# Splitting two of eight gate experts into two float32r parts, with an accumulating DMA that joins two output sums

## The chip, the cores and the metric

The kernel runs on one core of one Trainium2 chip. The metric is the device time of one execution in microseconds (us). Three runs of the kernel before gave 724.45, 724.79 and 724.89 us; their median, 724.79 us, is the time before. A separate execution was taken by the hardware profiler and is the source of every duration below.

## The reference, cut to what matters

The first half is a short dynamic convolution (seven taps, eight heads), the second a gated feed-forward layer. All of it is float32.

```python
w = softmax(weight_gen)                       # (4, 4160, 8, 7), over the 7 taps
out = einsum('bshk,bskhg->bshg', w, x_unf)    # x_unf: x at the 7 positions up to s; (4, 4160, 192)
h = maximum(out @ w_in, 0)                    # (4, 4160, 1024)
conv_out = sum_k conv_w[k] * h[s + k - 1]     # three taps along s, per channel
gate = 1 / (1 + exp(-conv_out))
result = (h * gate) @ w_out                   # (4, 4160, 192)
```

## The kernel before, in words

The 4 x 4160 positions are cut into 128 segments of 130 positions, one per partition. A **block** is four positions of every segment, so 512 tokens; there are 33 blocks (`NB`), the first with two positions of output and the others with four. The 1024 inner channels are eight groups of 128; the code calls one `f`, and it is called an expert here as in the change's title.

Each block goes through four stages:

1. **Attention** (`head`). Seven products of `x` (kept in a ring in SBUF) with the softmax weights, each 128 x 768, called taps (line 292), most on POOL. In the first three blocks TensorE transposes and adds all seven. From the fourth block on they are first folded: an accumulating DMA adds three pieces onto three others (`fold1`, line 315), a second one adds two onto two (`fold2`, line 318), POOL adds the last two (`fold3`, line 322), and TensorE transposes one piece, in two parts (line 327). POOL executes in order and issues both DMAs, so `fold2` waits on POOL until `fold1` has landed.
2. **First product** (`mm1`, line 359). The transposed block is split in a high and a low float32r part (lines 338 and 343). For each expert five float32r multiplications with 512 moving columns make `z`: one **unit**, eight a block.
3. **Gate** (lines 365 to 392). ACT takes the ReLU, ACT and VectorE make the three-tap convolution, ACT the tanh, and VectorE writes the gated value `g` (`gmul`) into an SBUF buffer of all eight experts.
4. **Second product** (`mm2`, line 405). For each of the block's 128-token slices eight float32 multiplications, one per expert, `g` as the weights and 192 columns of `w_out` as the moving side: one **tile**. There are 2 + 32 x 4 = 130. ACT evacuates a tile (line 414), and SP stores a block (line 418). The trace shows a float32 multiplication as two rows, each with a weight load of its own: 130 x 8 x 2 = 2080 rows.

Before this the weights arrive in an eight-byte form and are decoded on ACT, VectorE and POOL, which takes the first stage of the program; POOL there waits for VectorE through small memsets (`tok`, lines 874 and 875).

The order of all instructions comes from a planner in the kernel: `task(engine, duration, dependencies)` collects the work, a list scheduler with priorities (`TO` for attention, `FO` for transposes, `WO_` for tiles, in blocks) and one pass from the end and one from the start order it, and each engine then executes its part in that fixed order. `PLAN` and `SMX` say which taps and softmax steps go to VectorE (V) or POOL (G), `CH` and `WOE` do so for the decoding, and `FORD` is the order of the experts in the first block.

Of the kernel before, what the change touches and what calls it, by code (L numbers as in the profile page):

```python
# [33 lines left out]
NY = 2  # L34
NZ = 5
# [3 lines left out]
CG = 2  # L39
CH = (  # L40
    ("f", 0, 256, 5.2, "VVS", "V"),
    ("m", 0, 256, 8.7, "VVS", "G"),
    ("f", 256, 512, 17.0, "GGP", "G"),
    ("m", 256, 512, 16.0, "VVS", "V"),
    ("m", 512, 1024, 18.0, "VVP", "V"),
)
# [19 lines left out]
def kernel(  # L66
# [49 lines left out]
    wo = const.tile([P, NF, D], F32, name="wo")  # L116
# [232 lines left out]
    def geom(j):  # L349
        no = R if j else R - 2  # L350
        return no, R + 1 - no
# [9 lines left out]
    def hrow(f, a, n):  # L361
        return h[:, f, a:a + n, :].rearrange("p s t -> p (s t)")
# [22 lines left out]
    def g_of(j, f):  # L385
        if j not in g_t:
            g_t[j] = g_p.tile([P, NF, W], F32, tag="g", name="g")
        return g_t[j][:, f, :geom(j)[0] * P]

    def gmul(j, f):  # L390
        no, cc = geom(j)
        nc.vector.scalar_tensor_tensor(  # L392
            out=g_of(j, f), in0=z_t[j, f][:, :no * P], scalar=1.0, in1=hrow(f, cc, no), op0=ALU.add, op1=ALU.mult
        )

    def carry(f0):
# [4 lines left out]
    def mm2(j, i, ps=None):  # L401
        if ps is None:
            ps = (ps_d if i % 2 else ps_o).tile([P, W], F32, tag="dps" if i % 2 else "ops", name="ops")
        for f in range(NF):
            nc.tensor.matmul(  # L405
                out=ps[:, 0:D], lhsT=g_of(j, f)[:, i * P:(i + 1) * P], rhs=wo[:, f, :],
                start=(f == 0), stop=(f == NF - 1),
            )
        return j, i, ps

    def evac(j, i, ps):
        if i == 0:
            o_t[j] = o_p.tile([P, R, D], F32, tag="o", name="o")
        nc.scalar.activation(out=o_t[j][:, i, :], in_=ps[:, 0:D], func=ACTF.Copy, scale=0.5)  # L414

    def store(j, a, b):
        c0 = R * j - 2 if j else 0
        nc.sync.dma_start(
            out=os_[:, (c0 + a) * D:(c0 + b) * D], in_=o_t[j][:, a:b].rearrange("p s d -> p (s d)")
        )  # L420

    V, G = nc.vector, nc.gpsimd

    with tc.manual_schedule():
        stage = g_p.tile([P, NF, W], I32, tag="g", name="stage").rearrange("p f w -> p (f w)")
        r_in = stage[:, 0:2 * FF].rearrange("p (c b) -> p c b", b=2)
        r_fold = stage[:, 2 * FF:3 * FF].rearrange("p (c b) -> p c b", b=2)
        r_cw = stage[0:3 * NF, 3 * FF:3 * FF + 2 * P].rearrange("p (c b) -> p c b", b=2)
        r_out = [o_p.tile([P, 2 * D, 2], I32, tag="o", name="r_out") for _ in range(4)]
        w_in_i = w_in.bitcast(I32).rearrange("k (f b) -> k f b", b=2)  # L430

        def load_in(eng, kind, a, b):
# [73 lines left out]
        def dma(occ, deps, fn):  # L506
            return task("none", 3.2, [task("H", occ, deps, fn)])
# [118 lines left out]
        wo_rdy = []  # L626
        for c in range(4):
            w = 2 * D
            iB, iC = ((1, 2), (4, 5))[c % 2]
            j_, _ = dec(  # L630
                wo[:, 2 * c:2 * c + 2].rearrange("p c d -> p (c d)").bitcast(I32), r_out[c],
                slots[iB][:, 0:w], slots[iC][:, 0:w], dma(1.6, spreads, lambda c=c: load_out(c)), used((iB, iC)), WOE[c],
            )
            last_use[iB] = last_use[iC] = [j_]
            wo_rdy.append(j_)


# [5 lines left out]
        def dadd(deps, occ, fn, e):  # L643
            return task("none", 3.2, [task("D", occ, [task("G", e, deps, fn)])])
# [9 lines left out]
        def head(q):  # L654
# [48 lines left out]
            if yend:  # L703
                yf_.append(task("none", 0.0, yend))

        zl, last_mm, mm_end = [], [None], {}

        def unit(j, f):
            n = j * NF + f
            so = 1 if j else 0  # L710
            now[0] = j + (FORD.index(f) if j == 0 else f) / NF
            mm[n] = task(
                "P", 1.135, spl_done[j] + w_rdy[f] + zl[-NZ:][:1] * (len(zl) >= NZ), lambda: mm1(j, f), after=[last_mm[0]])
            last_mm[0] = mm_end[j] = mm[n]
            m_ = geom(j)[0] * P
            r_ = task("A", act(W), [mm[n], ca.get(n - NF)] + ([] if j else [c2]), lambda: relu(j, f))
            y_ = task("A", act(m_, 1) + 0.04, [r_, c2], lambda: wmid(j, f))
            cv_ = task("V", vec(m_), [y_], lambda: conv_side(j, f, 2, 1))
# [3 lines left out]
            rd[n] = gm[n] = task("V", vec(m_, 0), [t_] + dep, lambda: gmul(j, f))  # L722
# [8 lines left out]
        zfree, last_evac, stored = [], [], []  # L731

        def out_tiles(j):
            d_ = 0.03 + NF * 0.326
            no = geom(j)[0]
            for i in range(no):
                now[0] = j + WO_ + i / R
                hold = {}
                z_ = j == NB - 1 and i % 2 == 0

                def fn(i=i, hold=hold, z_=z_):
                    hold[0] = mm2(j, i, ps_z.tile([P, W], F32, tag="z", name="z") if z_ else None)
                dep = [mm[NU - 1], (zl + zfree)[-NZ]] if z_ else bank[1 + i % 2]
                a_ = tiles[j, i] = task(
                    "P", d_, [rd[j * NF + f] for f in range(NF)] + wo_rdy + dep, fn,
                    after=[tiles.get((j, i - 1))])
                e_ = task("A", act(D) + 0.02, [a_] + (stored[-4:][:1] if i == 0 and len(stored) > 3 else []),
                          lambda hold=hold: evac(*hold[0]), begun=last_evac)
                last_evac[:] = [e_]
                if z_:  # L750
# [157 lines left out]
```

## Time and profile before

| | us |
|---|---|
| median of three runs | 724.79 |
| profiled execution, its own time | 722.55 |
| its span, first to last instruction | 720.8 |
| TensorE (PE) busy | 693.8 (96%) |
| VectorE (DVE) busy | 633.2 (88%) |
| ScalarE (ACT) busy | 546.9 (76%) |
| GpSimd (POOL) busy | 503.8 (70%) |

The span is 1.75 us shorter than that execution's own time, and that time is 2.24 us below the median. The granted TensorE clock was 0.998 of full speed over the span. A busy time is a union of recorded durations, which overlap from one instruction to the next, so the pace of an engine is better read from the distance between two starts.

### The profile page before, as it was taken

To read this page: it belongs to the slowest core of one execution; us is meant where nothing else is said; L and a number is where in the kernel's file an instruction comes from. 1 tells how busy PE (TensorE), PEld (TensorE's weight loads), DVE (VectorE), ACT (ScalarE), POOL (GpSimd) and SP (SyncE) were. 2 spreads that over 40 slices of the span, in tenths; PEclk is the share of its full clock that TensorE was granted. 3 is DMA by queue.
4 is the path that set the end of the run, shared out by engine and by line. 5 is a ranking of instruction groups with operands and counts; after the bars stand their busy time and mean duration, and the time that the engine had idled before them with its cause. 6 is when DMAs were issued, how large, how long until landed. Compare 5 with 4: busy or idle time off the path is not lost.

```text
span 720.8 us, 10895 instructions
## 1 busy us (share of the span) xinstructions
PE 693.8 (96%) x3809; PEld 630.0 (87%) x3809; DVE 633.2 (88%) x981; ACT 546.9 (76%) x1049; POOL 503.8 (70%) x390
## 2 busy tenths in 40 slices
PE   2799999899999999999999999999999999999998
PEld 1678898799999999999999999999999999999998
DVE  6999997899998989989898988999888888888882
ACT  3397887787878778878787787778777777787872
POOL 3588998969888789888777687887767767810000
PEclk9999999999999999999999999999999999999999
DMA  7635999997999888888898788878887886862111
GB/s 230 174 111 119 215 216 228 208 238 167 222 204 211 195 196 190 180 194 199 199 209 196 177 188 178 197 185 202 201 189 185 187 191 133 175 150 77 69 48 45
DMA packets 70787, 127.59 MB, mean 177 GB/s; under 512 B 5046, under 2 KB 42573, under 8 KB 70732
## 3 DMA queue, kind: packets, MB, share of 16 engines
q0 software_dynamic: 20160, 58.99, 47.0%
q1 hardware_dynamic: 50090, 67.51, 28.3%
q8 instruction: 30, 0.49, 0.3%
q10 hardware_dynamic: 482, 0.40, 0.2%
q14 instruction: 25, 0.20, 0.1%
HBM read 20.51 MB, written 12.78 MB: 46 GB/s over the span
## 4 chain that ended last, share of the span: by engine, by line
PE 82%; POOL 10%; DMA 4%; issue 2%; DVE 1%; ACT 1%; SPq 0%; POOLq 0%
PE ops L405 41%; PE z L359 36%; POOL py L292 4%; POOL px L292 4%; PE tp L327 3%; DMA px<-py 2%; DMA ring<-in_x_dram 1%; POOL px L318 1%; PE z L405 1%; DMA stage<-in_moe_w_in_dram 1%; POOL px L322 0%; POOL px L315 0%; DVE px L292 0%; POOL w L242 0%; SPq L437 0%
## 5 line engine op out<-in xcount | busy, mean ns | idle before, releaser
L376 DVE SCALAR_TENSOR_TENSOR z<-h,cw,z 128x512 f32<-128x512 f32 (+1 forms) x528 | 377.6, 741 | 14.7 <-ACT z L369 10.5
L405 PE MATMUL ops<-wo,g 128*128 128x192 f32 x2048 | 353.2, 326 | 0.0
L405 PEld LDWEIGHTS ops<-wo,g 128*128 128x128 f32 x2048 | 338.8, 190 | 10.2 <-DVE H L343 0.4
L359 PE MATMUL z<-H,wi 128*128 128x512 f32 x1056 | 304.3, 410 | 3.4 <-DVE g L392 3.4
L292 POOL TENSOR_TENSOR px<-ring,w 128x768 f32<-128x768 f32 (+2 forms) x141 | 229.6, 1774 | 66.8 <-PE tp L327 66.5
L359 PEld LDWEIGHTS z<-H,wi 128*128 128x128 f32 x1056 | 191.9, 189 | 35.6 <-DVE g L392 4.4
L392 DVE SCALAR_TENSOR_TENSOR g<-z,h 128x512 f32<-128x512 f32 (+1 forms) x264 | 179.5, 681 | 34.7 <-ACT z L383 32.0
L383 ACT ACTIVATE z<-z 128x512 f32<-128x512 f32 (+1 forms) x264 | 152.1, 577 | 61.7 <-DVE z L376 60.6
L369 ACT ACTIVATE z<-h,cw 128x512 f32<-128x512 f32 (+1 forms) x264 | 180.1, 683 | 5.4
L365 ACT ACTIVATE h<-z 128x512 f32<-128x512 f32 x264 | 156.0, 592 | 34.1 <-PE z L359 33.7
L292 POOL TENSOR_TENSOR py<-ring,w 128x768 f32<-128x768 f32 (+2 forms) x109 | 167.8, 1852 | 0.0
L359 PE MATMUL z<-L,wi 128*128 128x512 f32 x264 | 103.4, 392 | 0.0
L322 POOL TENSOR_TENSOR px<-px 128x768 f32<-128x768 f32 x30 | 68.2, 2275 | 8.5 <-DMA px<-px 8.5
L318 POOL DMA_DIRECT2D px<-px x30 | 38.3, 1275 | 31.5 <-DMA px<-py 31.2
L359 PEld LDWEIGHTS z<-L,wi 128*128 128x128 f32 x264 | 49.7, 188 | 11.4
L338 ACT ACTIVATE H<-tp 128x512 fp32r<-128x512 f32 (+1 forms) x63 | 37.2, 591 | 25.5 <-PE tp L327 25.3
L327 PE MATMUL tp<-ident,px 128*128 128x128 f32 (+1 forms) x288 | 45.5, 282 | 6.6 <-POOL px L292 3.5
L414 ACT ACTIVATE o<-ops 128x192 f32<-128x192 f32 x128 | 41.8, 326 | 10.6 <-PE ops L405 10.4
L327 PEld LDWEIGHTS tp<-ident,px 128*128 128x128 f32 (+1 forms) x288 | 34.4, 133 | 15.0 <-POOL px L292 5.5
L315 POOL DMA_DIRECT2D px<-py x30 | 42.7, 1424 | 6.4 <-POOL py L292 6.3
L343 DVE TENSOR_TENSOR L<-tp,H 128x512 fp32r<-128x512 f32 x33 | 22.7, 688 | 13.5 <-ACT H L338 13.4
L343 DVE TENSOR_TENSOR H<-tp,H 64x512 fp32r<-64x512 f32 x30 | 20.5, 683 | 2.2 <-ACT H L338 1.3
(81 smaller groups left out, 187.0 us busy)
## 6 DMA issues: line engine op xcount, KB each, us to landing
px<-py POOLq DMA_DIRECT2D x30, 1152.0 KB, 10.5
h<-h SPq DMA_DIRECT2D x128, 256.0 KB, 4.9
px<-px POOLq DMA_DIRECT2D x30, 768.0 KB, 6.8
ring<-in_x_dram SPq DMA_DIRECT2D x31, 384.0 KB, 7.9
out_dram<-o SPq DMA_DIRECT2D x31, 384.0 KB, 6.9
w<-in_weight_gen_dram SPq DMA_DIRECT2D x15, 224.0 KB, 7.2
r_out<-in_moe_w_out_dram SPq DMA_DIRECT2D x4, 384.0 KB, 5.3
wi<-scr SPq DMA_DIRECT2D x8, 128.0 KB, 5.8
```

Of the source, the lines that this page charges most:

```text
L292: eng.tensor_tensor(out=dst[:, a:b, :].rearrange("p s (h g) -> p s h g", g=GRP), in0=ring[:, p:p + n, :].rearrange("p s (h g) -> p s h g", ...
L318: nc.gpsimd.dma_start(out=fl4(px_t[q][:, 0:2]), in_=fl4(px_t[q][:, 2:4]), accum_op=ALU.add, max_dma_last_dim=3072)
L322: nc.gpsimd.tensor_tensor(out=a, in0=a, in1=b, op=ALU.add)
L327: nc.tensor.matmul(dst[0:D2 if part else P, c * P:(c + 1) * P], lhsT=src[:, c, part * P:part * D2 + P], rhs=ident, is_transpose=True, star ...
L343: nc.vector.tensor_tensor(out=H[D2:P, :] if part else h_t[q, "L1"], in0=tp[r, :], in1=H[r, :].bitcast(F32), op=ALU.subtract)
L359: nc.tensor.matmul(out=z, lhsT=w[:, fs], rhs=h_t[j, nm], start=(i == 0), stop=(i == len(terms) - 1))
L365: nc.scalar.activation(out=hrow(f, 2, R), in_=z_t[j, f], func=ACTF.Relu)
L369: nc.scalar.activation(out=z_t[j, f][:, :no * P], in_=hrow(f, cc, no), func=ACTF.Copy, scale=cw[:, NF + f:NF + f + 1])
L376: nc.vector.scalar_tensor_tensor(out=z, in0=hrow(f, cc + d, no), scalar=cw[:, k * NF + f:k * NF + f + 1], in1=z, op0=ALU.mult, op1=ALU.add,)
L383: nc.scalar.activation(out=z, in_=z, func=ACTF.Tanh, scale=0.5)
L392: nc.vector.scalar_tensor_tensor(out=g_of(j, f), in0=z_t[j, f][:, :no * P], scalar=1.0, in1=hrow(f, cc, no), op0=ALU.add, op1=ALU.mult)
L405: nc.tensor.matmul(out=ps[:, 0:D], lhsT=g_of(j, f)[:, i * P:(i + 1) * P], rhs=wo[:, f, :], start=(f == 0), stop=(f == NF - 1),)
```

## The change

- Experts 0 and 1 (`NS = 2`) get float32r weights: `wos` holds, for each, a high part and a low part of `w_out` side by side. Their gate goes to a new buffer `gt`; ACT copies it to float32r (`gH`), and POOL subtracts to get the rest (`gL`). Per expert and tile, one float32r multiplication of `gH` with 384 columns (high and low) and one of `gL` with 192 columns (high) stand in place of one float32 multiplication. The other six stay float32.
- A tile's sum now lies in two halves of 192 columns: the low half of the weights has its own columns. ACT evacuates 384 columns instead of 192, and per block an accumulating DMA, issued by POOL (`join`), adds the one half to the other before the store. In the last block VectorE adds them (`evac2`).
- The output buffers are twice as large and three instead of four. The scratch of the decoding (`scr`) is gone: it lies in gate buffers, as does the staging of the weights.
- The planner's numbers change: a tap of the third block moves from VectorE to POOL, softmax steps of the third and fourth weight group change engine, decoding steps move, and `TO`, `FO`, `WO_` and `FORD` are new.

```diff
-    ("a", "GVVGGGG"),
+    ("a", "GGGVGGG"),
 )
-SMX = ("VV", "VV", "VV", "VG")
+SMX = ("VV", "VV", "GG", "VV")
-TO = -3.05
-FO = -0.65
-WO_ = 1.47
+TO = -2.15
+FO = -0.9
+WO_ = 1.97
...
-FORD = (1, 3, 2, 7, 0, 6, 5, 4)
+FORD = (1, 2, 4, 7, 0, 6, 3, 5)
+NS = 2
...
-    o_p = ctx.enter_context(tc.tile_pool(name="o", bufs=4))
+    gt_p = ctx.enter_context(tc.tile_pool(name="gt", bufs=2))
+    o_p = ctx.enter_context(tc.tile_pool(name="o", bufs=3))
...
+    def g_hi(j, f):
+        nc.scalar.activation(out=g_of(j, f, "gH"), in_=gt_t[j, f][:, :geom(j)[0] * P], func=ACTF.Copy)
+
+    def g_lo(j, f):
+        nc.gpsimd.tensor_tensor(
+            out=g_of(j, f, "gL"), in0=gt_t[j, f][:, :geom(j)[0] * P], in1=g_of(j, f, "gH").bitcast(F32),
+            op=ALU.subtract,
+        )
...
-        for f in range(NF):
+        t = slice(i * P, (i + 1) * P)
+        for f in range(NS):
             nc.tensor.matmul(
-                out=ps[:, 0:D], lhsT=g_of(j, f)[:, i * P:(i + 1) * P], rhs=wo[:, f, :],
-                start=(f == 0), stop=(f == NF - 1),
+                out=ps[:, 0:2 * D], lhsT=g_of(j, f, "gH")[:, t], rhs=wos[:, f].rearrange("p l d -> p (l d)"),
+                start=(f == 0), stop=False,
+            )
+            nc.tensor.matmul(
+                out=ps[:, 0:D], lhsT=g_of(j, f, "gL")[:, t], rhs=wos[:, f, 0, :], start=False, stop=False
+            )
+        for f in range(NS, NF):
+            nc.tensor.matmul(
+                out=ps[:, 0:D], lhsT=g_of(j, f)[:, t], rhs=wo[:, f - NS, :], start=False, stop=(f == NF - 1),
             )
...
+    def join(j):
+        n = geom(j)[0]
+        a, b = (o_t[j][:, i, 0:n].rearrange("p s d -> p (s d)") for i in range(2))
+        nc.gpsimd.dma_start(out=a, in_=b, accum_op=ALU.add)
...
-    scr = [const.tile([P, 3, W], I32, name=f"scr{i}") for i in range(2)]
+        s_a = g_p.tile([P, NP, W], I32, tag="g", name="s_a")
+        s_b = g_p.tile([P, NS, W], I32, tag="gH", name="s_b")
...
-                stored.append(dma(1.2, [e_], lambda: store(j, 0, no)))
+                stored.append(dma(1.2, [dadd([e_], 3, lambda: join(j), 0.62)], lambda: store(j, 0, no)))
```

What the order does is shown at three places. The first is one tile on TensorE, anywhere in the program. Before:

```order
L405 MATMUL ops<-wo,g 128x192 x8
```

and now:

```order
L427 MATMUL ops<-wos,gH 128x384
L431 MATMUL ops<-wos,gL 128x192
L427 MATMUL ops<-wos,gH 128x384
L431 MATMUL ops<-wos,gL 128x192
L435 MATMUL ops<-wo,g 128x192 x6
```

Two of the eight float32 multiplications became four float32r ones.

The second is POOL's queue early on, from the second `fold2` to the third `fold3` (block 5; `px<-px` as TENSOR_TENSOR is `fold3`, as DMA it is `fold2`, `px<-py` is `fold1`). Before:

```order
L318 DMA px<-px 128x2x768
L292 TENSOR_TENSOR py<-ring,w 128x768 x2
L322 TENSOR_TENSOR px<-px 128x768
L315 DMA px<-py 128x3x768
L292 TENSOR_TENSOR px<-ring,w 128x768
L322 TENSOR_TENSOR px<-px 128x768
```

and now, from the second `fold3` to the third:

```order
L326 TENSOR_TENSOR px<-px 128x768
L296 TENSOR_TENSOR px<-ring,w 128x768
L412 TENSOR_TENSOR gL<-gt,gH 128x512 x2
L296 TENSOR_TENSOR px<-ring,w 128x768
L322 DMA px<-px 128x2x768
L296 TENSOR_TENSOR py<-ring,w 128x768 x3
L319 DMA px<-py 128x3x768
L296 TENSOR_TENSOR px<-ring,w 128x768
L457 DMA o<-o 128x768
L326 TENSOR_TENSOR px<-px 128x768
```

Up to the third `fold3` the queue now holds, beyond what it held before, six subtractions of 512 columns, two of 256, three joins and one tap.

The third is POOL's queue in the middle of the program, from a `fold1` to the `fold2` that waits for it. Before:

```order
L315 DMA px<-py 128x3x768
L322 TENSOR_TENSOR px<-px 128x768
L292 TENSOR_TENSOR px<-ring,w 128x768
L264 TENSOR_TENSOR w<-w,r 128x448
L292 TENSOR_TENSOR px<-ring,w 128x768
L318 DMA px<-px 128x2x768
```

and now:

```order
L319 DMA px<-py 128x3x768
L412 TENSOR_TENSOR gL<-gt,gH 128x512
L457 DMA o<-o 128x768
L326 TENSOR_TENSOR px<-px 128x768
L296 TENSOR_TENSOR px<-ring,w 128x768 x4
L322 DMA px<-px 128x2x768
```

A subtraction, a join and two more taps stand between the two DMAs there.

## Rows read from the trace of the kernel before

**Rows 1.** Busy time by stretch: PE, PEld, DVE, ACT, POOL, PE clock, DMA share, GB/s.

```profile
0.00:40.00 40.00, 20.93 (x120) 17.27 (x120) 31.95 (x74) 15.91 (x38) 19.53 (x28) 0.96 0.69 202
...
80.00:120.00 40.00, 39.41 (x218) 35.67 (x218) 34.22 (x54) 30.16 (x58) 37.17 (x28) 1.00 1.02 227
...
160.00:200.00 40.00, 40.00 (x220) 36.53 (x220) 37.88 (x58) 32.36 (x63) 37.07 (x32) 1.00 0.87 201
```

**Rows 2.** Waits of PE: total us, times, longest.

```profile
PE tp L567 <- DVE tok L874: 12.7, 1, 12.7
PE tp L327 <- POOL px L292: 3.5, 3, 1.6
```

**Rows 3.** Timeline of PE in the middle: start, us, instruction.

```profile
404.51 0.60 PE L327 MATMUL tp<-ident,px 128*128 128x128 f32 x4
...
406.11 2.76 PE L405 MATMUL ops<-wo,g 128*128 128x192 f32 x16
408.71 0.60 PE L327 MATMUL tp<-ident,px 128*64 128x128 f32 x4
...
410.31 1.09 PE L359 MATMUL z<-H,wi 128*128 128x512 f32 x4
...
411.46 0.81 PE L405 MATMUL ops<-wo,g 128*128 128x192 f32 x4
...
424.98 0.60 PE L327 MATMUL tp<-ident,px 128*128 128x128 f32 x4
```

**Rows 4.** Groups by line: count, busy us, mean ns, idle before and its cause.

```profile
L405 PE MATMUL ops<-wo,g 128*128 128x192 f32 x2048 | 353.2, 326 | 0.0
L292 POOL TENSOR_TENSOR px<-ring,w 128x768 f32<-128x768 f32 (+2 forms) x141 | 229.6, 1774 | 66.8 <-PE tp L327 66.5
L365 ACT ACTIVATE h<-z 128x512 f32<-128x512 f32 x264 | 156.0, 592 | 34.1 <-PE z L359 33.7
L414 ACT ACTIVATE o<-ops 128x192 f32<-128x192 f32 x128 | 41.8, 326 | 10.6 <-PE ops L405 10.4
L318 POOL DMA_DIRECT2D px<-px x30 | 38.3, 1275 | 31.5 <-DMA px<-py 31.2
```

**Rows 5.** Timeline of POOL in the first stage, with the idle time before.

```profile
57.05 0.10 POOL L875 MEMSET tok<- 128x1 f32 x1 [5.15 <-DVE tok L874]
...
94.39 1.95 POOL L242 TENSOR_TENSOR w<-w,m 128x448 f32<-128x448 f32 x1
95.33 5.50 POOL L292 TENSOR_TENSOR px<-ring,w 128x768 f32<-128x768 f32 x3
...
106.49 1.85 POOL L322 TENSOR_TENSOR px<-px 128x768 f32<-128x768 f32 x1
...
113.61 1.83 POOL L322 TENSOR_TENSOR px<-px 128x768 f32<-128x768 f32 x1 [2.45 <-DMA px<-px]
```

**Rows 6.** Timeline of PE at the transposes of blocks 4 and 5.

```profile
108.39 0.66 PE L327 MATMUL tp<-ident,px 128*128 128x128 f32 x4
...
117.98 0.60 PE L327 MATMUL tp<-ident,px 128*128 128x128 f32 x4
```

**Rows 7.** Timeline of POOL in the middle.

```profile
399.13 2.28 POOL L322 TENSOR_TENSOR px<-px 128x768 f32<-128x768 f32 x1
400.92 1.73 POOL L315 DMA_DIRECT2D px<-py  x1
401.74 2.49 POOL L292 TENSOR_TENSOR px<-ring,w 128x768 f32<-128x768 f32 x1
403.24 1.91 POOL L242 TENSOR_TENSOR w<-w,m 128x448 f32<-128x448 f32 x1
```

**Rows 8.** DMA: the accumulating queue; fold1 by issue; one fold1 in the chain.

```profile
q0 software_dynamic: 20160, 58.99, 47.0%
...
px<-py POOLq DMA_DIRECT2D x30, 1152.0 KB, 10.5
...
108.24 13.48 DMA px<-py
```

More of the change, by code (lines that the diff above doesn't have):

```diff
@@ L115 @@
     wh, wl = wi[:, 0], wi[:, 1]
-    wo = const.tile([P, NF, D], F32, name="wo")
+    NP = NF - NS
+    wo = const.tile([P, NP, D], F32, name="wo")
+    wos = const.tile([P, NS, 2, D], F32R, name="wos")
     h = const.tile([P, NF, R + 2, P], F32, name="h")
@@ L383, in sig, with g_of @@
         nc.scalar.activation(out=z, in_=z, func=ACTF.Tanh, scale=0.5)
[L385 to L388, printed above, removed]
+    def g_of(j, f, nm="g"):
+        if (j, nm) not in g_t:
+            g_t[j, nm] = g_p.tile(
+                [P, NP if nm == "g" else NS, W], F32 if nm == "g" else F32R, tag=nm, name=nm)
+        return g_t[j, nm][:, f - NS if nm == "g" else f, :geom(j)[0] * P]
+    gt_t = {}
     def gmul(j, f):
         no, cc = geom(j)
-        nc.vector.scalar_tensor_tensor(
-            out=g_of(j, f), in0=z_t[j, f][:, :no * P], scalar=1.0, in1=hrow(f, cc, no), op0=ALU.add, op1=ALU.mult
+        if f >= NS:
+            dst = g_of(j, f)
+        else:
+            gt_t[j, f] = gt_p.tile([P, W], F32, tag="gt", name="gt")
+            dst = gt_t[j, f][:, :no * P]
+        nc.vector.scalar_tensor_tensor(
+            out=dst, in0=z_t[j, f][:, :no * P], scalar=1.0, in1=hrow(f, cc, no), op0=ALU.add, op1=ALU.mult
+        )
[5 more added lines that the diff above has]
+            op=ALU.subtract,
         )
@@ L412, in evac, with evac2 @@
         if i == 0:
-            o_t[j] = o_p.tile([P, R, D], F32, tag="o", name="o")
-        nc.scalar.activation(out=o_t[j][:, i, :], in_=ps[:, 0:D], func=ACTF.Copy, scale=0.5)
+            o_t[j] = o_p.tile([P, 2, R, D], F32, tag="o", name="o")
+        if j < NB - 1:
+            nc.scalar.activation(
+                out=o_t[j][:, :, i, :], in_=ps[:, 0:2 * D].rearrange("p (l d) -> p l d", l=2), func=ACTF.Copy, scale=0.5
+            )
+        else:
+            nc.scalar.activation(out=o_t[j][:, 0, i, :], in_=ps[:, 0:D], func=ACTF.Copy, scale=0.5)
+    def evac2(j, i, ps):
+        o = o_t[j][:, 0, i, :]
+        nc.vector.scalar_tensor_tensor(out=o, in0=ps[:, D:2 * D], scalar=0.5, in1=o, op0=ALU.mult, op1=ALU.add)
+    def join(j):
+        n = geom(j)[0]
+        a, b = (o_t[j][:, i, 0:n].rearrange("p s d -> p (s d)") for i in range(2))
+        nc.gpsimd.dma_start(out=a, in_=b, accum_op=ALU.add)
     def store(j, a, b):
@@ L418, in store @@
         nc.sync.dma_start(
-            out=os_[:, (c0 + a) * D:(c0 + b) * D], in_=o_t[j][:, a:b].rearrange("p s d -> p (s d)")
+            out=os_[:, (c0 + a) * D:(c0 + b) * D], in_=o_t[j][:, 0, a:b].rearrange("p s d -> p (s d)")
         )
@@ L424 @@
     with tc.manual_schedule():
[L425 to L429, printed above, removed]
+        r_in = g_p.tile([P, NP, W], I32, tag="g", name="r_in").rearrange("p f w -> p (f w)")
+        r_cw = r_in[0:3 * NF, 2 * FF:2 * FF + 2 * P].rearrange("p (c b) -> p c b", b=2)
+        r_in = r_in[:, 0:2 * FF].rearrange("p (c b) -> p c b", b=2)
+        r_st = g_p.tile([P, NS, W], I32, tag="gL", name="r_st").rearrange("p f w -> p (f w)")
+        r_fold = r_st[:, 0:FF].rearrange("p (c b) -> p c b", b=2)
+        s_a = g_p.tile([P, NP, W], I32, tag="g", name="s_a")
+        s_b = g_p.tile([P, NS, W], I32, tag="gH", name="s_b")
+        r_o = [o_p.tile([P, 2, 2 * D, 2], I32, tag="o", name="r_o") for _ in range(2)]
+        r_out = [t[:, i] for t in r_o for i in range(2)]
         w_in_i = w_in.bitcast(I32).rearrange("k (f b) -> k f b", b=2)
@@ L576 @@
         w_rdy, last_use = {f: [] for f in range(NF)}, {i: [] for i in range(6)}
-        slots = [t[:, i] for t in scr for i in range(3)]
+        slots = [s_a[:, i] for i in range(4)] + [s_b[:, i] for i in range(2)]
         def used(ix):
@@ L628 @@
             w = 2 * D
+            sp = 2 * c < NS
             iB, iC = ((1, 2), (4, 5))[c % 2]
-            j_, _ = dec(
-                wo[:, 2 * c:2 * c + 2].rearrange("p c d -> p (c d)").bitcast(I32), r_out[c],
-                slots[iB][:, 0:w], slots[iC][:, 0:w], dma(1.6, spreads, lambda c=c: load_out(c)), used((iB, iC)), WOE[c],
+            j_, bits = dec(
+                None if sp else wo[:, 2 * c - NS:2 * c + 2 - NS].rearrange("p c d -> p (c d)").bitcast(I32), r_out[c],
+                slots[iB][:, 0:w], slots[iC][:, 0:w], dma(1.6, spreads, lambda c=c: load_out(c)), used((iB, iC)),
+                "VVP" if sp else WOE[c],
             )
             last_use[iB] = last_use[iC] = [j_]
+            if sp:
+                ends = []
+                for k in range(2):
+                    f = 2 * c + k
+                    d3 = lambda bits=bits, k=k: bits().bitcast(F32)[:, k * D:(k + 1) * D]
+                    if f >= NS:
+                        ends.append(task("A", act(D), [j_], lambda f=f, d3=d3: nc.scalar.activation(
+                            out=wo[:, f - NS, :], in_=d3(), func=ACTF.Copy)))
+                        continue
+                    a_ = task("A", act(D), [j_], lambda f=f, d3=d3: nc.scalar.activation(
+                        out=wos[:, f, 0, :], in_=d3(), func=ACTF.Copy))
+                    ends.append(task("V", vec(D), [a_], lambda f=f, d3=d3: V.tensor_tensor(
+                        out=wos[:, f, 1, :], in0=d3(), in1=wos[:, f, 0, :].bitcast(F32), op=ALU.subtract)))
+                j_ = task("none", 0.0, ends)
+                dbank[0] = ends
             wo_rdy.append(j_)
@@ L704, in head @@
                 yf_.append(task("none", 0.0, yend))
+        gtl = []
         zl, last_mm, mm_end = [], [None], {}
@@ L733, in out_tiles @@
         def out_tiles(j):
-            d_ = 0.03 + NF * 0.326
+            d_ = 0.03 + NP * 0.326 + NS * 0.284
             no = geom(j)[0]
```

14 lines of the change are left out of this document (10 added, 4 removed).

## The prediction

> **What bounds the kernel now.** I read the busy times by stretch first [rows 1]. From 160 us on PE is busy for all of every 40 us at a granted clock of 1.00, which is the upper of its two levels (2.4 GHz). In the first 40 us it is busy for 20.93, and at 80 to 120 us, where the DMA engines show a share of 1.02, for 39.41. The waits of PE [rows 2] agree: one of 12.7 us at the very start, then a few on POOL, none later. So after the first stage the kernel is bound by PE, and the other engines count only while they keep up. The timeline shows the pace: the transposes of two neighbouring blocks start at 404.51 and 424.98 us, 20.47 us a block [rows 3]. In the groups [rows 4], POOL's largest wait, 66.5 us, is for buffers that PE has to free: in the middle POOL runs ahead.
>
> Early on it does not. Block 4's `fold3` starts at 106.49 us and PE, which waited, takes its result at 108.39; block 5's starts at 113.61 and lasts to 115.44, and PE comes at 117.98, 2.54 us later [rows 5, 6].
>
> **What the change saves on PE.** A tile lasts 408.71 - 406.11 = 2.60 us for 16 rows, 0.1625 each; a float32 multiplication is two, 0.325 us [rows 3]. The new pair (384 columns, then 192) stands in no trace of before, so I bound it.
>
> - The 384 columns. A unit of five 512-column float32r steps lasts 411.46 - 410.31 = 1.15 us, 0.230 a step [rows 3]. By columns 384 take 0.173. That step cannot be dearer than 0.230; at the low end I put one row of the float32 tile, 0.163.
> - The 192 columns. The nearest row is a transpose, which has its own weight load and 128 columns: four of them and a unit last 406.11 - 404.51 = 1.60 us, so four last 0.45, 0.113 each [rows 3]. Half a row of the float32 tile, 0.081, is the low end; the high end is a whole float32 multiplication, 0.325, if few columns lose the fast rate.
>
> I take 0.173 + 0.113 = 0.286, as the transpose is the nearest in size and alone shows how fast weight loads can follow each other. The ends are 0.244 and 0.555. There are 130 tiles with two pairs, so 260 x (0.325 - 0.286) = **10.1 us less**, and a block of 20.47 - 8 x 0.039 = 20.16 us.
>
> [...]
>
> **What the change adds beside PE.**
>
> - ACT, a block: two copies of 512 columns, 0.592 us each as the ReLU; and four evacuations of 384 columns instead of 192. On the line through 0.326 us for 192 and 0.592 for 512 [rows 4] that is 0.16 more each. Together 1.8 us, so ACT's 546.9 us of busy time become some 606 in about 714, 85%. Covered by PE; it would show only if ACT passed 20.16 us a block.
> - VectorE: the gate product is as long as before, and six POOL and VectorE moves fall in the first stage. Nothing in the middle.
> - POOL, a block before: seven taps of 403.24 - 401.74 = 1.50, `fold3` 400.92 - 399.13 = 1.79, two DMA issues of 401.74 - 400.92 = 0.82, one softmax step of 95.33 - 94.39 = 0.94: 14.9 us [rows 5, 7]. Added: two subtractions. They are nearest to `fold3`, also two operands in SBUF, at 2/3 of its columns: 1.19 each; the ends are 1.0 (a tap by columns) and 1.79. And a join's issue, 0.82. Sum 14.9 + 3.2 = 18.1 us in 20.16, plus the waits for `fold1`, 31.2 us over 30 blocks [rows 4], 1.0: 19.1. Covered, with 1 us to spare; this is the thinnest cover.
> - What waits behind a waiting instruction: `gL` waits for ACT's copy, the join for the evacuation, and behind them on POOL are the taps. SP's store now waits for the join, with the carry of `h` and the load of `x` behind it, needed most of a block later. I price these at nothing as long as POOL's cover holds.
> - DMA: the accumulating queue moved 58.99 MB in 47.0% of the span [rows 8], 338.8 us, 5.74 us a MB. A join of 0.39 MB is 2.3 us a block. The share of 0.87 at 160 to 200 us [rows 1] is 17.8 us of 20.47; with the join 20.1 of 20.16. By rate it fits: 201 GB/s there become (201 x 20.47 + 393) / 20.16 = 224, and 227 was moved at 80 to 120 us [rows 1]. Transfers will take longer, and how long decides a rival.
>
> **The first stage.** Ahead of block 5's `fold3` POOL's queue holds more: one tap and one of two 256-column subtractions (0.6 us each by columns) stand ahead of the last wait for VectorE, 5.15 us at 57.05 [rows 5], and fit into it. Behind it are six subtractions of 1.19, one of 0.6 and three joins of 0.82: 10.2 us. Of these POOL's idle 2.45 us before that `fold3` [rows 5] take some, PE's lateness there 2.54 us, and PE has three units more and the same 11 tiles, each cheaper, ahead of that point: 3 x 1.15 - 11 x 0.078 = 2.6 us. What is left, 10.2 - 2.45 - 2.54 - 2.6 = **2.6 us, is new waiting of PE**. Later POOL gains 1 us a block on PE and is no longer late. The ends are 0 (other idle time takes it too) and 10.2 (none does).
>
> **The end.** After the last tile VectorE must add the halves: as ACT's copy of 192 columns, 0.326 us [rows 4], and a hand-over, **0.4 us**. The join and store of the block before end under the last four tiles, 4 x 2.52 us.
>
> **Sum.** -10.1 + 2.6 + 0.4 = -7.1 us. Against the profiled execution's own 722.55 that is 715.4; its median of runs stands 2.24 higher, so 724.79 - 7.1 = **717.7 us**.
>
> **The rivals.**
>
> 1. *The pair is cheaper.* Both parts at their low ends, 0.244 us: 260 x 0.081 = 21 us less, with 3 us for the start and the end 706.8. For it: the float32 rows repeat at 0.1625 us with a weight load each. Against it: float32r steps of 512 columns take 0.230, not the 0.216 to be had by columns from that row. Chance 0.12.
> 2. *POOL's start is not absorbed.* All 10.2 us arrive at PE: 724.79 - 10.1 + 10.2 + 0.4 = 725.3, no difference. For it: `fold3` of block 4 is taken at once today [rows 5, 6]. Against it: the idle times above. Chance 0.13, from 722.5 to 727.
> 3. *The folds bind; slower.* The place is POOL's wait at `fold2`. From `fold1`'s issue to there the new queue holds 0.82 + 1.19 + 0.82 + 1.79 + 4 x 1.50 = 10.6 us of work, and a `fold1` lands after 10.5 (median); but where the DMA share was full one took 13.48 [rows 8]. Then POOL waits 2.9 us in each block and needs 18.1 + 2.9 = 21.0 against PE's 20.16; it has no lead left from the start, so 28 blocks cost 28 x 0.8 = 23 us: 740. It decides from a landing of 10.6 + (20.16 - 18.1) = 12.7 us on. For it: the share of 1.02, and the sum of 20.1 us above. Against it: shares count packets that overlap, and a slower POOL asks for fewer transfers. The Trainium skill, page DMA: Bandwidth & Descriptors, section Issuing engines are not separate DMA queues, has all transfers run on the same 16 engines, which speaks for it. Chance 0.16, from 727 to 750.
> 4. *The 192-column multiplication has the float32 rate.* The pair takes 0.173 + 0.325 = 0.498 us, 260 x 0.173 = 45 us more: 724.79 + 45 + 3 = 773. No row shows a float32r step under 512 columns, so it cannot be excluded; nothing speaks for it. Chance 0.05. Two float32r steps then cost more than the one they replace.
>
> **How the numbers follow.** The forecast has the remaining 0.54; its own range is 714 to 723, from 0 to 7.6 us for the start. A measurement can tell 0.2%, 1.4 us, from no change. Below 723.4: the forecast, rival 1 and a sixth of rival 2, 0.68. Within: about half of rival 2 and a little of 3, 0.08. Above: the rest, 0.24. For eight in ten the range starts at 706, which takes in the centre of rival 1, and ends at 731, which leaves out most of rival 3 and rival 4, 0.19.
>
> **What would show it.** Right: the float32r pair repeats every 0.28 to 0.29 us, transposes of neighbouring blocks start 20.1 to 20.2 us apart from 200 us on with no wait of PE, and PE waits some 3 us more than before between 60 and 130 us. Wrong: a pair under 0.26 or over 0.31; PE waiting for POOL's `fold3` after 200 us, with POOL waiting over 2 us a block for `fold1`; or a first stage as short as before.

## The result and the profile after

The changed kernel took **733.03 us** (median of 4 runs, 732.26 to 734.65) beside 724.84 of the kernel before (724.45 to 725.26): a ratio of 1.0116, interval 1.0098 to 1.0134. It is slower by 8.2 us, where 7.1 us less than before were forecast, and lies outside the range of 706 to 731. The profiled execution took 732.26 us with a span of 730.2.

The chain that ended last, by engine, on the profile's page of the kernel before:

```profile
PE 82%; POOL 10%; DMA 4%; issue 2%; DVE 1%; ACT 1%; SPq 0%; POOLq 0%
```

The page of the changed kernel: busy time of the engines, the accumulating queue (packets, MB, share of 16 engines) and the chain.

```profile
PE 688.9 (94%) x3809; PEld 617.9 (85%) x3809; DVE 624.1 (85%) x986; ACT 593.3 (81%) x1117; POOL 617.9 (85%) x491
q0 software_dynamic: 24768, 71.37, 54.1%
POOL 39%; PE 28%; DMA 13%; DVE 10%; issue 5%; ACT 5%; POOLq 0%; DVEq 0%; ACTq 0%
```

PE held 82% of the chain; now the longest part is POOL's, 39%. POOL's busy time rose from 503.8 us to 617.9. The stretches say when it matters (columns as in [rows 1]):

```profile
0.00:40.00 40.00, 19.00 (x113) 16.34 (x114) 29.62 (x72) 15.01 (x35) 22.33 (x30) 0.91 0.70 196
...
80.00:120.00 40.00, 38.70 (x212) 34.19 (x211) 34.42 (x54) 33.16 (x63) 39.52 (x32) 1.00 1.01 220
...
160.00:200.00 40.00, 38.56 (x214) 34.58 (x213) 33.02 (x51) 32.11 (x60) 38.08 (x30) 1.00 1.01 226
...
360.00:400.00 40.00, 38.14 (x210) 34.03 (x209) 35.00 (x54) 34.46 (x65) 38.48 (x30) 1.00 0.89 197
...
600.00:640.00 40.00, 40.00 (x223) 36.19 (x222) 35.94 (x54) 35.21 (x66) 39.13 (x30) 1.00 0.94 201
```

```profile
160.00:560.00 400.00, 386.83 (x2127) 346.43 (x2126) 348.51 (x529) 337.90 (x631) 383.94 (x297) 1.00 0.94 212
```

From 160 us on PE should have been busy for all of each 40 us, as before [rows 1]. It is not, until 560 us, and POOL is busy for 38 to 39 of the 40 us in the rows from 160 us on. What PE waits for in 160 to 560 us (total us, times, longest), the list of waits says:

```profile
PE tp L331 <- POOL px L326: 9.1, 7, 1.9
PE z L363 <- DVE g L404: 2.2, 3, 1.0
PE tp L331 <- DVE L L347: 0.9, 1, 0.9
PE z L363 <- DVE gt L404: 0.8, 2, 0.6
```

Line 326 is `fold3`, line 331 the transposes: PE comes to a block's transposes and `fold3` is not done. Before, PE had no wait after 160 us, and the largest on POOL were 3.5 us for its products [rows 2].

The saving itself is there. PE's timeline where it is bound by itself (start, us, instruction): two pairs, twelve float32 rows, and the transposes of two neighbouring blocks.

```profile
601.29 0.33 PE L427 MATMUL ops<-wos,gH 128*128 128x384 f32 x1
601.46 0.25 PE L431 MATMUL ops<-wos,gL 128*128 128x192 f32 x1
601.55 0.36 PE L427 MATMUL ops<-wos,gH 128*128 128x384 f32 x1
601.75 0.25 PE L431 MATMUL ops<-wos,gL 128*128 128x192 f32 x1
601.83 2.14 PE L435 MATMUL ops<-wo,g 128*128 128x192 f32 x12
...
650.37 0.60 PE L331 MATMUL tp<-ident,px 128*128 128x128 f32 x4
...
670.54 0.60 PE L331 MATMUL tp<-ident,px 128*128 128x128 f32 x4
```

A block takes 20.17 us of PE, 0.30 less than 20.47 [rows 3]; eight pairs a block, so a pair costs 0.325 - 0.30 / 8 = 0.2875. Over 260 pairs that is 9.8 us. In 160 to 560 us PE's time not busy is 13.2 us where it was none, and by the distances of its starts (a recorded duration covers part of a wait) 17 us: the saving is more than gone. Roughly, -9.8 + 17 + 0.4 for the end + 0.75 for 60 to 160 us (PE busy for 96.40 us there, before for 97.15) make +8.4; the span grew by 9.4 (730.2 - 720.8), so 1 us is not placed. The start is not where it went: in the first 40 us PE does less than before, but over the first 60 us it was busy for 39.00 us, before for 38.97.

POOL's timeline at the two ends of the stretch, the `fold3` of blocks 7 and 23:

```profile
167.08 1.81 POOL L326 TENSOR_TENSOR px<-px 128x768 f32<-128x768 f32 x1
...
487.62 1.80 POOL L326 TENSOR_TENSOR px<-px 128x768 f32<-128x768 f32 x1
```

Sixteen blocks in 320.54 us, **20.03 us a block**. That is less than the 20.17 that PE takes for a block. But the order asks faster there: in the run without the join (below), where PE hardly waited, its transposes of blocks 7 and 23 start 19.26 us apart per block. The order lets PE take new blocks ahead of output tiles: behind block 32's transposes 59.7 us of the span are left (730.2 - 670.54), where the order before left 720.8 - 670.58 = 50.2.

### The profile page after: what moved, and what is told of

Read it like the earlier page. It is cut to its first block, busy times and chain, and to the rows that moved or that the text cites. A ratio compares the mean times of both kernels' runs of the same rounds, so it can differ in the third digit from the quotient of the medians.

```text
span 730.2 us, 11227 instructions
## 1 busy us (share of the span) xinstructions
PE 688.9 (94%) x3809; PEld 617.9 (85%) x3809; DVE 624.1 (85%) x986; ACT 593.3 (81%) x1117; POOL 617.9 (85%) x491
## 3 DMA queue, kind: packets, MB, share of 16 engines
q0 software_dynamic: 24768, 71.37, 54.1%
## 4 chain that ended last, share of the span: by engine, by line
POOL 39%; PE 28%; DMA 13%; DVE 10%; issue 5%; ACT 5%; POOLq 0%; DVEq 0%; ACTq 0%
POOL py L296 12%; PE z L363 11%; POOL px L296 11%; PE ops L435 11%; DMA px<-py 9%; DVE z L380 4%; POOL gL L412 4%; POOL px L326 4%; POOL px L322 3%; DMA h<-h 2%; POOL px L319 2%; PE ops L427 2%; POOL o L457 2%; ACT h L369 1%; DVE g L404 1%
## 5 line engine op out<-in xcount | busy, mean ns | idle before, releaser
L435 PE MATMUL ops<-wo,g 128*128 128x192 f32 x1536 | 273.5, 328 | 0.0
L435 PEld LDWEIGHTS ops<-wo,g 128*128 128x128 f32 x1536 | 246.3, 190 | 0.0
L296 POOL TENSOR_TENSOR px<-ring,w 128x768 f32<-128x768 f32 (+1 forms) x142 | 243.7, 1991 | 0.6
L296 POOL TENSOR_TENSOR py<-ring,w 128x768 f32<-128x768 f32 (+2 forms) x109 | 185.8, 2105 | 0.0
L412 POOL TENSOR_TENSOR gL<-gt,gH 128x512 fp32r<-128x512 f32 (+1 forms) x66 | 110.0, 1879 | 40.4 <-ACT gH L409 40.4
L404 DVE SCALAR_TENSOR_TENSOR g<-z,h 128x512 f32<-128x512 f32 (+1 forms) x198 | 130.7, 677 | 15.2 <-ACT z L387 6.9
L427 PE MATMUL ops<-wos,gH 128*128 128x384 f32 x256 | 82.2, 358 | 0.0
L444 ACT ACTIVATE o<-ops 128x384 f32<-128x384 f32 x126 | 60.8, 485 | 24.3 <-PE ops L435 23.4
L431 PE MATMUL ops<-wos,gL 128*128 128x192 f32 x256 | 64.2, 251 | 0.0
L322 POOL DMA_DIRECT2D px<-px x30 | 46.9, 1565 | 13.3 <-DMA px<-py 12.9
L404 DVE SCALAR_TENSOR_TENSOR gt<-z,h 128x512 f32<-128x512 f32 (+1 forms) x66 | 44.8, 680 | 10.9 <-POOL gL L412 5.4
## 6 DMA issues: line engine op xcount, KB each, us to landing
px<-py POOLq DMA_DIRECT2D x30, 1152.0 KB, 10.2
```

The costliest lines, as they stand in the source:

```text
L296: eng.tensor_tensor(out=dst[:, a:b, :].rearrange("p s (h g) -> p s h g", g=GRP), in0=ring[:, p:p + n, :].rearrange("p s (h g) -> p s h g", ...
L404: nc.vector.scalar_tensor_tensor(out=dst, in0=z_t[j, f][:, :no * P], scalar=1.0, in1=hrow(f, cc, no), op0=ALU.add, op1=ALU.mult)
L412: nc.gpsimd.tensor_tensor(out=g_of(j, f, "gL"), in0=gt_t[j, f][:, :geom(j)[0] * P], in1=g_of(j, f, "gH").bitcast(F32), op=ALU.subtract,)
L427: nc.tensor.matmul(out=ps[:, 0:2 * D], lhsT=g_of(j, f, "gH")[:, t], rhs=wos[:, f].rearrange("p l d -> p (l d)"), start=(f == 0), stop=False,)
L435: nc.tensor.matmul(out=ps[:, 0:D], lhsT=g_of(j, f)[:, t], rhs=wo[:, f - NS, :], start=False, stop=(f == NF - 1),)
```

## The experiments

The first four runs separated the parts. Theories named in the expectations: "early asking" (the order asks too soon), "slow transfers" (the join's bytes delay the folds), "first stage" (POOL never recovers from its start), and the rival that POOL is the bound whatever the order.

**No join.** In `join`, with all else in place:

```diff
-        nc.gpsimd.dma_start(out=a, in_=b, accum_op=ALU.add)
+        return
```

> The changed kernel in the same order, but POOL issues no join: the product with the low part of the two experts' output weights is left out of the sums. Theory 'early asking' (POOL takes 19.95 us a block between blocks 7 and 23, the fixed order of PE asks for one every 18.96 us, and PE pays the difference): POOL loses one issue of 0.62 us a block and some waiting, comes down to about 19.1, and most of the 17 us that PE waited between 160 and 560 us go: 717 to 721 us. Theory 'slow transfers' (the join's 0.39 MB a block lengthen the folds and POOL waits for their landing): the folds land as before the change, POOL's waits fall to under 1 us a block, about 715 to 718 us. Theory 'first stage' (the new numbers of the planner cost at the start): no change, 731 to 733.

Measured: **715.88 us**, ratio 0.9888 (0.9868 to 0.9908). The trace of this run: 160 to 560 us (columns as in [rows 1]) and, there, the one wait of PE for `fold3`.

```profile
160.00:560.00 400.00, 397.84 (x2210) 360.85 (x2209) 361.42 (x548) 350.66 (x653) 380.82 (x291) 1.00 0.87 200
```

```profile
PE tp L331 <- POOL px L326: 1.8, 1, 1.8
```

The timelines of POOL at `fold3` and of PE at the transposes, of blocks 7 and 23:

```profile
164.47 2.75 POOL L326 TENSOR_TENSOR px<-px 128x768 f32<-128x768 f32 x1
...
472.94 1.85 POOL L326 TENSOR_TENSOR px<-px 128x768 f32<-128x768 f32 x1
```

```profile
168.68 0.60 PE L331 MATMUL tp<-ident,px 128*128 128x128 f32 x4
...
476.88 0.60 PE L331 MATMUL tp<-ident,px 128*128 128x128 f32 x4
```

The time lies in the range of "slow transfers", but not for its reason: POOL's waits for the landings of `fold1` and `fold2` in 160 to 560 us are 8.0 and 1.1 us here, and 5.5 and 1.3 in the changed kernel. Without the join POOL needs 19.28 us a block and the whole cost of 17 us is gone. Subtraction, copies, wide evacuations, order and first stage are all still there: "first stage" falls, and so does any theory that leaves the join out.

**No subtraction.** `g_lo` left out, a constant zero taken as its result:

```diff
     def g_lo(j, f):
-        nc.gpsimd.tensor_tensor(
...
+        return
...
-                out=ps[:, 0:D], lhsT=g_of(j, f, "gL")[:, t], rhs=wos[:, f, 0, :], start=False, stop=False
+                out=ps[:, 0:D], lhsT=glc[:, f, t], rhs=wos[:, f, 0, :], start=False, stop=False
...
+        glc = g_p.tile([P, NS, W], F32R, tag="gL", name="glc")
+        nc.vector.memset(glc.bitcast(F32), 0.0)
```

> The changed kernel in the same order, with the joins, but POOL makes no subtraction: TensorE multiplies a constant buffer of zeros as the low part of the two gates, so that part is left out of the sums while TensorE's work is the same. Theory 'early asking': POOL loses 2.5 us a block, 17.5 is under the 18.96 that PE asks for, no wait of PE after 160 us: 714 to 717. Theory 'slow transfers': the transfers stay, POOL still waits for landings, at least half of the loss stays: 723 to 731. Theory 'first stage': 731 to 733.

Measured: 725.24 us, ratio 1.0027 (1.0011 to 1.0043). POOL had 2.2 us a block less to do, and only some 7 us came back. Its waits in 160 to 560 us show where the rest went:

```profile
POOL px L322 <- DMA px<-py: 26.7, 11, 5.9
POOL px L326 <- DMA px<-px: 11.1, 7, 4.6
```

In the changed kernel these two were 5.5 and 1.3 us. A POOL with less to do waits for `fold1` and `fold2` instead, in transfers that share the DMA engines with the join. So there are two bounds close together: POOL's own length, and the folds' landing.

**The planner counts POOL longer**, by 5 per cent, which changes the order:

```diff
+            dur = dur * 1.05 if eng == "G" else dur
```

> The changed kernel whole, with one thing changed in the planner: it counts every POOL instruction 5% longer, so that PE's order asks for a block every 20.0 us between blocks 7 and 23 instead of 18.96 (320 us of PE work between their transposes instead of 303); POOL's work is the same. Theory 'early asking': POOL's 19.95 us suffice, PE's waits after 160 us fall from 17 us to under 3: 715 to 720 us. A rival, 'POOL is the bound whatever the order': PE's waits only move, 729 to 735. 'Slow transfers' says the same as that rival: the transfers are the same, 729 to 735.

Measured: 734.72 us, ratio 1.0143 (1.0114 to 1.0172). This run alone proved little: its first 40 us held 12.58 us of PE's work where the change's held 19.00. So it was run again with the longer count only for work ranked after block 2:

> The changed computation whole; the planner counts POOL's instructions 5 per cent longer, but only for work that it ranks after block 2, so that the first 135 rows of TensorE's order are the change's own. In the earlier run with 5 per cent from the first instruction on, TensorE's waits after 160 us were half the change's, but its first 40 us held 6.4 us less of TensorE's work. 'Order' (what the order asks of POOL counts, and the lost start hid it): 724 to 729 us. 'POOL and the folds are the bound whatever the order': 731 to 735 us.

Measured: 732.93 us, ratio 1.0115 (1.0087 to 1.0143), with 18.91 us of PE's work in the first 40 us. In both of these orders PE has one whole block of work, 20.17 us, for every block from 7 to 23. Yet the `fold3` of these blocks start 20.72 us apart in the first and 20.80 in the second, whose rows are these:

```profile
170.02 2.89 POOL L326 TENSOR_TENSOR px<-px 128x768 f32<-128x768 f32 x1
...
502.79 2.12 POOL L326 TENSOR_TENSOR px<-px 128x768 f32<-128x768 f32 x1
```

So POOL itself went slower than the 20.03 us of the change's order: in 160 to 560 us of the second run it waited 8.6 us for `fold2` to land instead of 1.3, and 9.7 for VectorE's part of the softmax instead of 5.0. PE's time not busy there fell from 13.2 to 6.2 us, but 60 to 160 us held 2.6 us less of its work (93.84 against 96.40), and the time stayed. "Early asking" alone falls, as far as these two orders can tell; why POOL goes slower in them stays open.

**VectorE adds the halves** in every block, as the change does in the last; no join, and the planner told so:

```diff
...
-                if j == NB - 1:
+                if True:
                     e_ = task("V", vec(D), [e_], lambda hold=hold: evac2(*hold[0]))
...
-                stored.append(dma(1.2, [dadd([e_], 3, lambda: join(j), 0.62)], lambda: store(j, 0, no)))
+                stored.append(dma(1.2, [e_], lambda: store(j, 0, no)))
```

> The changed kernel with the two halves added by VectorE from PSUM in every block, as the change does in the last one, and ACT evacuating 192 columns as before; no join by DMA, the planner told so and free to reorder. Its order asks for a block every 18.9 us from block 7 to 23 (302 us of PE work), with about 17.1 us of POOL work for each instead of 18.0. 'Early asking': POOL at 19.0 to 19.3 with its waits, little left of PE's waiting: 715 to 722. 'Slow transfers': 715 to 718, POOL's waits for landings under 1 us a block. 'First stage': 731 or more.

Measured: 723.9 us, ratio 0.9995 (0.9985 to 1.0005), which lies in none of the three readings. From 280 us on PE did not wait, but an early wait cost twice (timeline of PE, then busy time, columns as in [rows 1]):

```profile
89.85 1.12 PE L331 MATMUL tp<-ident,px 128*128 128x128 f32 x4 [2.70 <-POOL px L326]
```

```profile
92.00:98.00 6.00, 5.62 (x24) 5.37 (x25) 4.93 (x9) 1.79 (x5) 4.08 (x4) 0.64 0.61 165
```

Behind the wait four transposes take 1.12 us on the record instead of 0.60, and the granted clock of the six us from 92 us on is 0.64: part of them at the lower level (1.2 GHz), after PE had stood idle.

**What in the join costs.** Three runs in the change's own order: a join of one of the four rows; the whole join into the other half, so that the store does not wait for it; and a plain copy there.

```diff
# one row
-        n = geom(j)[0]
+        n = 1
# aside
-        nc.gpsimd.dma_start(out=a, in_=b, accum_op=ALU.add)
+        nc.gpsimd.dma_start(out=b, in_=a, accum_op=ALU.add)
# copy aside
-        nc.gpsimd.dma_start(out=a, in_=b, accum_op=ALU.add)
+        nc.gpsimd.dma_start(out=b, in_=a)
```

> The joining DMA moves one of the four rows of a block (three rows of the low-weight product never reach the output); its issue on POOL, its wait for the evacuations and the store's wait for it stay, and so does the order of every engine. Without any join the same order took 715.9 us, with the whole join 733.0. Theory 'bytes' (the 384 KB that the join takes through the DMA engines delay the folds): 4.3 us of those 17 are left, 718 to 723 us, and TensorE waits for fold3 after 160 us for less than 5 us. Rival 'POOL' (the issue of 0.62 us a block and the in-order wait on an engine that is already full): 729 to 735 us. Rival 'store' (SyncE, held by a store that waits for the join, issues the carries and x loads behind it late): the small join lands in half the time, 720 to 727 us.

> The joining DMA runs the other way, adding the high-weight half into the low-weight half, so that the store does not wait for it (the low-weight product never reaches the output). Bytes, queue, issue on POOL and its wait stay. 'Bytes': 729 to 735 us, as the change. 'POOL': 729 to 735 us. 'Store': 715 to 721 us, and the waits of the copies into h for the carries fall back to a few us over the program.

> As the run before, but the DMA copies instead of adding (the low-weight product never reaches the output). Same bytes over the fabric from POOL's queue, same issue, no store waiting. If the cost lies in the adding in the DMA engines' write (theory 'adding'): 716 to 722 us and a landing well under that of the join, 9.2 us. If it lies in the bytes whatever is done with them: 727 to 735 us. 'POOL': 729 to 735 us.

The copy again, issued by SyncE (SP in the rows):

```diff
-        nc.gpsimd.dma_start(out=a, in_=b, accum_op=ALU.add)
+        nc.sync.dma_start(out=b, in_=a)
```

> The copy of 384 KB a block from the high-weight half into the low-weight half, as in the run with the copy from POOL's queue (723.4 us), but issued by SyncE (the low-weight product never reaches the output). Order, bytes and the wait for the evacuations stay; only POOL's issue of 0.62 us a block is gone, and the copy is in another queue. 'POOL' (the issue is what the plain copy cost against the run without a join, 715.9): 715 to 718 us. 'Bytes': 721 to 726 us. A result between says that both count.

Measured, with the distance of the `fold3` starts of blocks 7 and 23 on POOL over 16, and PE's time not busy in 160 to 560 us. Each ratio is to runs of the kernel before that were taken beside that run; the differences below are nearly the same by the ratios as by the times.

| run | us | ratio to before (interval) | POOL, us a block | PE not busy |
|---|---|---|---|---|
| no join | 715.88 | 0.9888 (0.9868 to 0.9908) | 19.28 | 2.2 |
| copy by SyncE | 717.1 | 0.9903 (0.9884 to 0.9923) | 19.33 | 2.8 |
| copy by POOL | 723.4 | 0.9987 (0.9978 to 0.9996) | 19.69 | 5.8 |
| one row joined | 726.16 | 1.0025 (1.0014 to 1.0036) | 19.82 | 7.8 |
| join aside | 733.6 | 1.0127 (1.0112 to 1.0142) | 20.06 | 13.9 |
| the change | 733.03 | 1.0116 (1.0098 to 1.0134) | 20.03 | 13.2 |

The store's wait costs nothing: with and without it the time is the same, so that the one-row run, which by its time alone would suit that reading, is explained otherwise. 393 KB copied a block by SyncE cost 1.2 us in all, which the intervals do not tell from nothing, so bytes alone are not it.

The same copy issued by POOL costs 6.3 us more, and lies between its readings. It stands in the queue of the folds now, but they land no later for it. `fold1` and `fold2` with the copy by SyncE, then by POOL (issues, KB each, median us to landing):

```profile
px<-py POOLq DMA_DIRECT2D x30, 1152.0 KB, 10.4
px<-px POOLq DMA_DIRECT2D x30, 768.0 KB, 7.5
```

```profile
px<-py POOLq DMA_DIRECT2D x30, 1152.0 KB, 9.8
px<-px POOLq DMA_DIRECT2D x30, 768.0 KB, 7.4
```

Nor do POOL's waits in 160 to 560 us have one for the evacuations. What is left is the issue itself, on an engine with hardly a gap. POOL's timeline in the changed kernel shows it: 0.62 us from a join's start to the next start.

```profile
102.69 1.91 POOL L457 DMA_DIRECT2D o<-o  x1
103.31 3.16 POOL L326 TENSOR_TENSOR px<-px 128x768 f32<-128x768 f32 x1
```

The adding form costs another 10.2 us. What it takes of the DMA engines stands on the pages of the profile. No join, copy by POOL, one row joined and join aside:

```profile
q0 software_dynamic: 20160, 58.99, 46.4%
```

```profile
q0 software_dynamic: 22704, 71.37, 50.2%
```

```profile
q0 software_dynamic: 24768, 62.13, 48.9%
```

```profile
q0 software_dynamic: 24768, 71.37, 53.9%
```

Shares times span: 331.9, 362.0, 354.4 and 394.6 us. So 31 copies take 30 us of all 16 engines and 31 joins 63, 1.0 and 2.0 us each. The joins go in more packets (24,768 - 20,160 = 4,608, the copies in 2,544), but that is not all: one row goes in the same 4,608 and takes 22.5 us, and the other 9.2 MB take 40 more, 4.4 us a MB, where the whole copy takes 2.4.

Between copy and join, the median landing of `fold1` goes from 9.8 to 10.2 us and that of `fold2` from 7.4 to 7.8. How much of the 10.2 us of the kernel's time runs through these landings was not tried apart; one row, with a quarter of the bytes, cost 2.8 us more than the whole copy, so the adding does not go by bytes alone there either.

**Three steps of 192 columns instead of the pair**, with no second half and no join:

```diff
...
-                out=ps[:, 0:2 * D], lhsT=g_of(j, f, "gH")[:, t], rhs=wos[:, f].rearrange("p l d -> p (l d)"),
...
+            for l in range(2):
...
+                    out=ps[:, 0:D], lhsT=g_of(j, f, "gH")[:, t], rhs=wos[:, f, l, :],
...
```

> No join and no second half: the low weight part is multiplied by its own 192-column step into the same columns, so that each split expert takes three float32r steps of 192 columns (gH with the high weight, gH with the low weight, gL with the high weight) in place of one of 384 and one of 192. The whole computation. Measured from this: the price of a 192-column float32r step. If it is 0.087 us, as from the gL step to the next in the changed kernel's timeline, a triple takes 0.26 us and the time is 708 to 713 us (run without the join: 715.9, less 256 times 0.026). If a step takes 0.115 us (the pair's 0.286 less the 0.171 from gH to gL), a triple takes 0.345 and the time is 727 to 733 us. The theories on the join say nothing of the price, but all of them expect that TensorE does not wait for fold3 after 160 us for more than 5 us.

Measured: 730.34 us, ratio 1.0082 (1.0065 to 1.0099). PE hardly waited, and its own pace was slower:

```profile
647.35 0.60 PE L331 MATMUL tp<-ident,px 128*128 128x128 f32 x4
...
667.94 0.60 PE L331 MATMUL tp<-ident,px 128*128 128x128 f32 x4
```

20.59 us a block against 20.17: three steps cost 0.2875 + 0.42 / 8 = 0.34 us, 0.113 each. Same columns as the pair, one weight load more.

**Other orders for the version with VectorE.** The transposes ranked 0.15 of a block later (`FO = -0.75`), POOL counted 5 per cent longer, loads and taps ranked 0.25 of a block earlier (`TO = -2.4`), and the longer count only behind blocks 2 and 4:

> The version with VectorE adding the halves (723.9 us) lost its time in two places: TensorE waited 2.7 us for fold3 at 87 us, after which its clock was granted at 0.91 in that stretch, and 2 us in 200 to 240 us; from 280 us on it never waited. Here the planner ranks the transposes 0.15 of a block later; whole computation. If those waits are an accident of the order: 715 to 719 us. If VectorE's load (91 per cent) is what costs: 722 to 727 us.

> The same version with the planner counting POOL's instructions 5 per cent longer; whole computation. Accident of the order: 715 to 719 us. VectorE's load: 722 to 727 us. If POOL's length in the planner is what makes the early fold late, this one is the best of the three: 714 to 717 us.

> The same version with the planner ranking each block's loads, taps and folds 0.25 of a block earlier; whole computation. Accident of the order: 715 to 719 us. VectorE's load: 722 to 727 us.

> VectorE adds the halves, whole computation; POOL counted 5 per cent longer for work ranked after block 2 only. With 5 per cent from the start the run took 721.6 us, and its first 40 us held 6.2 us less of TensorE's work than without (12.6 against 18.8). If the start is all that this version lost: 715 to 718 us. If the order from block 2 on loses in another place: 719 to 725 us.

> As the run before, with the longer count from block 4 on. If the start is all: 715 to 718 us. If the wait at 87 us, with the lower clock behind it, belongs to the order before block 4: 720 to 724 us.

Measured: 732.13, **721.56** (ratio 0.9967, 0.9955 to 0.9979), 725.27, 722.15 (0.9977) and 722.31 us (0.9973). The first fell outside both of its readings, and the second just outside all three of its own. Three of the five beat both kernels, the best by 0.33% over the kernel before; none reached the 715 to 719 that an accident of the order would have given back. In the best run PE lost its time at the start (its waits over the whole span; ahead of these stands one of 12.8 us at the very start, as before [rows 2]):

```profile
PE tp L331 <- DVE px L296: 10.6, 1, 10.6
PE tp L331 <- POOL tok L943: 3.3, 1, 3.3
PE tp L331 <- POOL px L326: 2.8, 2, 1.7
```

With the longer count only behind block 2 or 4 the start was whole again (18.44 and 20.10 us of PE's work in the first 40), and waits came elsewhere before 160 us. The spread of 11 us over planner numbers says how far such an order decides; whether VectorE's load or the orders hold these back stays open.

**Softmax steps from POOL to VectorE**, with the join (`SMR = "VV"`):

> The changed computation whole, with the join; the two softmax steps that POOL takes for every second block (about 1.9 us of POOL, 0.95 a block) go to VectorE instead, from the fifth group of weights on. 'POOL alone is the bound': its 20.03 us a block fall to 19.1, as much as without the join, 716 to 721 us. 'Two bounds, POOL's length and the folds' transfers with the join between them' (the run without the subtraction relieved POOL of 2.2 us a block and kept the transfers, 725.2 us, POOL waiting for fold1): 724 to 729 us. VectorE too full (85 per cent before): over 730 us.

Measured: 740.29 us, ratio 1.0221 (1.0204 to 1.0239); only the last reading has the time, and that VectorE is too full is not shown: it is busy for 87% of the span, in the changed kernel for 85%. The small memsets by which POOL waits for VectorE (line 946) rose from 9 to 33, and POOL's waits at them from 18.8 to 36.2 us. POOL's waits in this run, over the whole span:

```profile
POOL px L322 <- DMA px<-py: 47.2, 13, 5.7
POOL tok L946 <- DVE tok L945: 36.2, 16, 6.5
```

Its waits for `fold1` were 12.9 us in the changed kernel. POOL was relieved and waited more, as in the run without the subtraction.

## Why the prediction was wrong

- **The pair, 0.286 us**: right. It measured 0.2875, the block 20.17 against 20.16. The transpose as the nearest row for a short step with its own weight load held: the three-step run gives 0.113. Rivals 1 and 4 fall.
- **ACT covered at 85%**: right, 81%. **The end, 0.4 us**: nothing in the trace speaks against it.
- **"Covered, with 1 us to spare; this is the thinnest cover"**: here the prediction failed. POOL's work of 18.1 us a block was well priced; by the distances of its starts it is 17.8. But its waits were taken as 1.0 us, from the one group for `fold1`. The distances put them at 2.2 a block, before `fold2`, `fold3`, both issues and the softmax step: together 20.03, not 19.1. Without the join they are as long (17.8 less the issue of 0.62 is 17.2, and 19.28 - 17.2 = 2.1), so the join does not make them; the forecast counted less than half of them. And the sum was held against 20.16, the mean pace of PE, when the order asked for a fold every 19.26 us in blocks 7 to 23. At 19.28, without the join, POOL just keeps up; at 20.03 it loses 0.75 us a block, 12 us over 16 blocks. That an order which asks every 20.17 us would have been covered is not shown: in the two orders that did, POOL took 20.72 and 20.80.
- **The join, "2.3 us a block" of DMA, "by rate it fits"**: the rate was right: 2.0 us measured, and 226 GB/s in the fullest stretch shown, where 224 were forecast. But fitting by rate did not make it free: the adding DMA cost 10.2 us over a copy, the issue on POOL 6.3.
- **"Later POOL gains 1 us a block on PE and is no longer late"**: wrong for the reason above. The first stage's own part, 2.6 us of new waiting, was not the trouble. PE's listed waits between 60 and 130 us rose by about that, from 0.5 to 3.6 us, but only 1.0 of them is for `fold3`; by 160 us 0.75 us of it is left (96.40 us of PE's work in 60 to 160 us against 97.15 before).
- **Rival 3, "the folds bind; slower"**, had the right side and a wrong place. POOL did not stand at `fold2`, as it named (5.5 us over 400, not 2.9 a block), as `fold1` landed after 10.2 us (median) and not after the 12.7 from which this rival decides; it was full of work. The folds do bind once POOL is relieved, as two runs showed. A rival "POOL's length, against what the order asks" was missing.

## What to carry to other kernels

An in-order engine covered "with 1 us to spare" of 20 may not be covered: add its waits from the distances of its starts, and hold the sum against the pace at which the order asks in that stretch, not only against the mean. An order that asks later is not a sure cure: the engine's waits change with the order. A DMA is not free when its bytes fit: ask which engine issues it and what else that engine has to do in the same microseconds. A cheap test is the same transfer issued elsewhere, or as a plain copy, in the same order.

## What the runs showed of the hardware that was not expected

An accumulating DMA inside SBUF of 393 KB took 2.0 us of all 16 engines, a plain copy of the same bytes from the same queue 1.0; the landings were 9.3 and 8.0 us. Three float32r steps of 192 columns cost 0.34 us where one of 384 and one of 192 cost 0.2875, so a 192-column step with weights of its own goes at 0.113 us, where by columns from the 512-column step (0.230) it would be 0.086.
